# Attention and SwiGLU on one core: first head pair loaded as f32 over the hardware queues, three probability buffers, and a new order for the first sixth of the work list

## Chip, cores, metric

One core of a Trainium2 chip. The metric is the device time of one execution in microseconds. Profiles are one execution each, and their spans are about 2 us below the timed figures.

## The reference

Eight batches of causal attention (8 heads of 64, 576 tokens, 16 beacon keys that every token sees), whose output, heads side by side, goes through a SwiGLU block of width 1536.

```python
B, H, S, Nb, D = (8, 8, 576, 16, 64)
k_all = np.concatenate([beacon_k, k], axis=2)
v_all = np.concatenate([beacon_v, v], axis=2)
scores = scale * np.matmul(q, k_all.transpose(0, 1, 3, 2))      # causal mask on k, none on beacons
a = np.exp(scores - max); a /= a.sum(-1, keepdims=True) + 1e-09
x = np.matmul(a, v_all)                                          # -> (4608, 512)
g = x @ w_gate
out = (g * sigmoid(g) * (x @ w_val)) @ w_out
```

## The kernel before

All work is cut into pieces, and a string, the work list, gives their order of issue: `S` scores of half a head pair with their Exp, `P` probabilities times V for one head (PV), `K`/`Q` transposes of batch 0, `U` of batches 1 and 2, `X` transposes of the attention output, `g`/`G` quarters and whole units of the gate and value products, `F` one step of the output projection, `l` a load, `o` half of Wo, `c`/`d` a regrouping copy of a K or Q head pair of batch 0, `t` a DMA transpose, `w` four idle transposes. The same letter in the other case (`k`, `q`, `x`, `u`, `D`) is the same piece with its copy out on another engine; `g` and `G` alone differ in size. TensorE takes its part of the list strictly in order.

```python
pt = [static.tile([P, 2, P_W], BF16, name=f"p{i}") for i in range(2)]     # probabilities, by head pair m % 2
...
nc.vector.memset(pt[1][:, 0, 0:TOK], 0.0)
for h0, h1 in ((0, 2),):
    load_runs(nc.gpsimd, ks, k, 0, h0, h1)        # f32 in HBM -> bf16 in SBUF
    load_runs(nc.gpsimd, qs, q, 0, h0, h1)
nc.gpsimd.dma_start(beacons[:], beacon_k[0].rearrange("h j d -> j h d"))
make_identity(nc, ident)
...                                               # mask tile "below"
warm(13, TOK)                                     # 13 idle 128x512 matmuls
...
start = runs(2, 4) + runs(4, H) + v_loads(0, 0, H)   # then weights, batch 1
...
plan = [
    "llllllllllllllllllllllllllllllllllloo",
    "cdwwwwkQ",
    "ScDKSQ",
    "cDcDSKPSQP",
    "SKPXSQP",
    ...
```

From batch 2 on, the masks of the diagonal blocks are put on by GpSimd (`affine_select` on the probabilities after Exp), which also issues nearly all loads.

The softmax here doesn't subtract the row's maximum and nothing guards it: scores larger than these inputs give would overflow.

Of the kernel before, what the change touches and what calls it, by code (L numbers as in the profile page):

```python
# [10 lines left out]
BF16 = mybir.dt.bfloat16  # L11
FP32 = mybir.dt.float32

P = 128
S = 576
D = 64
NB = 16
NKT = 5
KPAD = NKT * P
TOK = 512  # L20
# [9 lines left out]
RP = S // ROWS  # L30

NHT = 2

PE_MASKS = (0, 1)

# [21 lines left out]
def kernel(  # L57
# [40 lines left out]

    QK = NKT * H * D
    QKP = ROWS * H * D  # L100
    qs = static.tile([P, QKP], BF16, name="qs")
    ks = static.tile([P, QKP], BF16, name="ks")
    beacons = static.tile([NB, H, D], BF16, name="beacons")
    qb = [static.tile([P, n], BF16, name=f"qb{i}") for i, n in ((0, QKP), (1, QK))]
    kb = [static.tile([P, n], BF16, name=f"kb{i}") for i, n in ((0, QKP), (1, QK))]
    vb = [static.tile([P, NKT, H, 68], BF16, name=f"vb{i}") for i in range(2)]
    qT = [static.tile([P, NPAIR, KPAD], BF16, name=f"qT{i}") for i in range(2)]
    kT = [static.tile([P, NPAIR, KPAD], BF16, name=f"kT{i}") for i in range(2)]
    pt = [static.tile([P, 2, P_W], BF16, name=f"p{i}") for i in range(2)]
    wg = static.tile([P, KD, DFF], BF16, name="wg")  # L110
    wv = static.tile([P, KD, DFF], BF16, name="wv")
    wo = static.tile([P, NF, DM], BF16, name="wo")
# [3 lines left out]
    def tiles(t):  # L116
        return t[:, 0:QK].rearrange("p (c h d) -> p c h d", c=NKT, d=D)

    def load_runs(eng, t, src, b, h0, h1):
        eng.dma_start(  # L120
            t[0:RP, ROWS * D * h0 : ROWS * D * h1].rearrange("p (h e) -> p h e", e=ROWS * D),
            src[b, h0:h1].rearrange("h (p i) d -> p h (i d)", i=ROWS),
        )

    loaded = {}
# [56 lines left out]
    def copy(eng, o, i):  # L182
        if eng is nc.scalar:
            nc.scalar.activation(o, i, ACT.Copy)
        else:
            nc.vector.tensor_copy(o, i)  # L186

    def transpose_pair(dst, src, n, m, pool, tag, eng):
        t_ps = pool.tile([P, KPAD], BF16, name="t_ps", tag=tag)
# [53 lines left out]
    def scores(b, m, units):  # L243

        on_pe = b in PE_MASKS
        tiles = {u: big.tile([P, 2, 512], FP32, name="s_ps", tag="big") for u in units}
        for u in units:
            for t, col, q0, n in UNITS[u][2]:
                for hh in range(2):
                    r = slice(64 * hh, 64 * hh + 64)  # L250
                    nc.tensor.matmul(  # L251
                        tiles[u][:, hh, col : col + n],
                        lhsT=kT[b % 2][r, m, P * t : P * t + P],
                        rhs=qT[b % 2][r, m, q0 : q0 + n],

                        start=not on_pe or col == 0,
                        stop=not on_pe,
                    )
        if on_pe:
            for u in units:  # L260
                for hh in range(2):
                    for col, n, d in UNITS[u][3]:
                        nc.tensor.matmul(  # L263
                            tiles[u][:, hh, col : col + n],
                            lhsT=below[:],
                            rhs=ident[:, d : d + n],
                            start=False,
                            stop=(col, n, d) == UNITS[u][3][-1],
                        )
        for u in units:  # L270
            c0, w, _, diagonals = UNITS[u]
            p = pt[m % 2]
            nc.scalar.activation(p[:, :, c0 : c0 + w], tiles[u][:, :, 0:w], ACT.Exp, scale=0.125)  # L273
            for col, n, d in [] if on_pe else diagonals:
                ap = p[:, :, c0 + col : c0 + col + n]
                nc.gpsimd.affine_select(  # L276
                    out=ap,
                    in_=ap,
                    compare_op=ALU.is_ge,
                    fill=0.0,  # L280
                    base=d,
                    pattern=[[0, 2], [1, n]],
                    channel_multiplier=-1,
                )
# [3 lines left out]
    def pv(b, m, hh, pool=att, tag="att"):  # L288
# [4 lines left out]
        for c, (q0, _) in enumerate(QBLOCKS):  # L293
            for t in range(c + 1):
                col = p_col(t, q0)
                nc.tensor.matmul(  # L296
                    o_ps[:, c, 0 : D + 1],
                    lhsT=pt[m % 2][:, hh, col : col + P],
                    rhs=vb[b % 2][:, t, h, 0 : D + 1],
                    start=(t == 0),  # L300
                    stop=(t == c),
                )
# [118 lines left out]


    nc.vector.memset(pt[1][:, 0, 0:TOK], 0.0)
    for h0, h1 in ((0, 2),):
        load_runs(nc.gpsimd, ks, k, 0, h0, h1)
        load_runs(nc.gpsimd, qs, q, 0, h0, h1)
    nc.gpsimd.dma_start(beacons[:], beacon_k[0].rearrange("h j d -> j h d"))
    make_identity(nc, ident)

    nc.gpsimd.memset(below[:], 0.0)  # L430
    nc.gpsimd.affine_select(
# [13 lines left out]
                idle[:, 0:cols], lhsT=pt[1][:, 0, 0:P], rhs=pt[1][:, 0, 0:cols], start=True, stop=True  # L445
            )

    warm(13, TOK)
    for i in range(2):
        nc.vector.memset(vb[i][:, :, :, D : D + 1], 1.0)  # L450
        nc.vector.memset(vb[i][64:P, 4, :, 0:D], 0.0)
        nc.vector.memset(kT[i][:, :, NB + S : KPAD], 0.0)
        nc.vector.memset(pt[i][:, :, 1664:P_W], 0.0)
    def kq_loads(b):

        k, q = k_loads(b, 0, H), q_loads(b, 0, H)
# [5 lines left out]



    done = dict.fromkeys("SPKQUXgGFcdltwo", 0)
    first = [(0, 0, 1), (0, 1, 2), (1, 0, 1), (1, 1, 2), (0, 2, 3), (1, 2, 3), (0, 3, 4), (1, 3, 4)]
    parts = [(j, *part) for j in range(2) for part in first]
    units = [(j, f) for j in range(NCH) for f in range(2 if j < 2 else 0, NF)]
# [11 lines left out]
    def kq_then(b):  # L480
        return [(load, b, False) for load in kq_loads(b)]

    def runs(h0, h1):
        return [lambda t=t, src=src: load_runs(nc.gpsimd, t, src, 0, h0, h1) for t, src in ((ks, k), (qs, q))]

    start = runs(2, 4) + runs(4, H) + v_loads(0, 0, H)
    for i in range(4):
        start += w_loads(i)
    start += k_loads(1, 0, H) + q_loads(1, 0, H) + v_loads(1, 0, H)
# [10 lines left out]
        return outp, "outp"  # L500

    def piece(kind):
        n = done[{"k": "K", "q": "Q", "u": "U", "x": "X", "D": "d"}.get(kind, kind)]
        eng = nc.scalar if kind in "kqx" else nc.vector
        if kind == "S":
            b, m = n // 8, n % 8 // 2
            assert done["P"] >= 2 * (n // 2) - 2
            if b == 0:
                assert min(done["K"], done["Q"]) > m
            else:  # L510
# [1 line left out]
            scores(b, m, ("AB", "DC" if b == 0 else "CD")[n % 2])  # L512
        elif kind == "P":
            b, m = n // 8, n % 8 // 2
            assert done["S"] >= 2 * (n // 2 + 1) and loaded[b, "v"] == 6
            pv(b, m, n % 2, *small())
            if b >= NPEX and n % 8 == 7:
                x_transpose(b)
# [3 lines left out]
                assert loaded[key] == (2 if key[1:] == (True, 0) else 1)  # L522
            transpose_both(bt, n % 4, (nc.scalar if kind == "u" else nc.vector, nc.vector))
        elif kind in "KkQq":
            assert done["c" if kind in "Kk" else "d"] > n
            turn = transpose_k if kind in "Kk" else transpose_q
            turn(n, *small(), eng)
        elif kind in "Xx":
# [18 lines left out]
        elif kind == "o":  # L547
            load_wo(n)
        elif kind == "w":
            spare.extend(range(4))  # L550
        elif kind == "c":
            assert done["l"] >= (0, 2, 4, 4)[n]
            regroup(kb[0], ks, n, nc.vector)
        elif kind in "dD":
            assert done["l"] >= (0, 2, 4, 4)[n]
            regroup(qb[0], qs, n, nc.scalar if kind == "d" else nc.vector)
        elif kind == "l":
            load, b, values = loads[n]
            assert free(b, values)
            load()  # L560
        elif kind == "t":
            assert done["S"] >= 8 * (n // 10 + NPE - 1)
            turns[n]()
        done[{"k": "K", "q": "Q", "u": "U", "x": "X", "D": "d"}.get(kind, kind)] += 1

    one_bank = [(outp, "outp")]
    two_banks = [(outp, "outp"), (att, "att")]
    plan = [
        "llllllllllllllllllllllllllllllllllloo",
        "cdwwwwkQ",  # L570
        "ScDKSQ",
        "cDcDSKPSQP",
        "SKPXSQP",
        "SPXSP",
        "gPgPgxXgg",
        "gggGGGGGUlGGGGUGllllll",
        "llF",
        "FFSFFS",
        "USPlFFlSPUFX",
        "lUSPFSPUFXlllFF",  # L580
        "SlPllllllFlSPUUtXFF",
        "lllllS",
        "tPggSPFFggXlgltgtPttlgtFlgGFt",
        "lltllGFSlFltFFFSllPlGlFG",
        "llSPFFGFllSPFlF",
        "GSFFFPGStFFPFGGtF",
        "PStFPFSGFFPFSlFFFFFFtStt",
        "lFllllFFltltP",
        "StFtSPGlPGFGG",
        "FPSFFlFlFFSFGlFFllPFGlFFS",  # L590
        "FPFFlFFSllFPFGGGlltlFtFtFt",
        "PSFlFFFtSFFFlFFlPGGlGFFFlFF",
        "tFPStFFlttFSFlPFFGlGGFFFlFlF",
        "SFPSFFlFtFFGPFGGFFFFFF",
        "lSllPFFFtSlllPFFGFGGFFFFFFttt",
        "ltFlSlPFFtFSllPFFGFGGFFFFFtttt",
        "llSPFFFSllPFFFGGGFFFFFF",
        "SllPFFFSPFFFGGGFFFFFF",
        "SPFFFSPFFFGGGFFFFFFttttt",
        "SPFFFSPFFFGGGFFFFFFttttt",  # L600
        "SllPFFFSllPFFFGGGFFFFFF",
        "SllPFFFSPFFFGGGFFFFFF",
        "SPFFFSPFFFGGGFFFFFF",
        "PFSFFFSPFFGFFGGFFFF",
        "SPFFFFSPFFGGFFFFF",
        "SPFFFFSPFGFFGGFFFFFF",
        "GFFPGFFFFGGPFFF",
        "GGFFFFFFFFFGFFFFFFFF",
        "FFFFFFFFFFFFFFF",
        "GFFFFFGFFFFGFGFFFFGFFFFFGFFFFFFFGFFFFGFFGFFGGFFF",  # L610
        "GFFFGFFGGFFGFFFFFFFFFFFFFGFFGFFFGFFFFFFFGFFGFFGFFFFFFGFFGFFF",
        "FFFFFFFFFFFFFFFFFFFFFFFFFFFFFFFFFFFFFFFFFFFFFFFFF",
    ]
    for kind in "".join(plan).replace(" ", ""):
        piece(kind)
    del done["w"]
    assert done == dict(S=8 * B, P=8 * B, K=4, Q=4, U=4 * (NPE - 1), X=4 * NPEX, g=16, G=len(units), F=4 * NF * NCH, c=4, d=4, o=2, l=len(loads), t=len(turns)), done


# [28 lines left out]
```

## Time and profile before

| | before |
|---|---|
| time, median (range) | 389.08 us (389.08 to 389.61, 3 runs) |
| span of the profiled run | 387.0 us |
| TensorE busy | 370.9 us (96%) |
| start of first useful transpose, first Exp | 7.67, 10.03 us |
| last PV of batch 0 ends | 31.4 us |
| first scores of batch 2 | 72.9 us |
| from there to the end | 314.1 us |

Times within a span are us from its first instruction. The lines behind these figures are in the prediction. The moment "first scores of batch 2" matters because the two work lists are the same from just before it.

### The profile page before, as it was taken

The numbers are of one execution on the slowest core, as the hardware profiler recorded it, in microseconds if no ns is written. First come the engines' busy times: TensorE is split into PE (matmuls) and PEld (weight loads), VectorE is DVE, ScalarE is ACT, GpSimd is POOL, SyncE is SP. The second block draws the span as 40 slices with busy tenths as digits, with TensorE's granted clock in tenths as the row PEclk, the third lists the DMA queues.
The fourth block names the chain that finished last, engine by engine and source line by source line (L and its number), as shares of the span: only waits on it lengthen the run. The fifth ranks groups of instructions, "written<-read, shape, count | busy, mean of one in ns | idle before, by whom it ended". The sixth has DMA issues, their size and how long they took to land.

```text
span 387.0 us, 7394 instructions
## 1 busy us (share of the span) xinstructions
PE 370.9 (96%) x2885; PEld 185.7 (48%) x2933; DVE 231.1 (60%) x430; ACT 169.2 (44%) x242; POOL 156.2 (40%) x270
## 2 busy tenths in 40 slices
PE   7799999999989999999999999999999999999996
PEld 3564446644445454454444444444444444444443
DVE  3456866575654666656666666665666636675652
ACT  2563346655565555555454455555552112222210
POOL 8847949589229676537633114311110000000000
PEclk9679999999999999999999999999999999999999
DMA  7999999999549999999995158722000311000013
GB/s 91 173 203 165 150 168 147 177 135 135 72 69 123 157 105 150 197 77 68 180 173 75 41 112 138 73 41 76 29 27 29 61 73 37 27 29 27 29 56 109
DMA packets 158660, 38.73 MB, mean 100 GB/s; under 512 B 146592, under 2 KB 154144, under 8 KB 158624
## 3 DMA queue, kind: packets, MB, share of 16 engines
q0 software_dynamic: 112864, 19.15, 67.6%
q1 hardware_dynamic: 45616, 19.03, 24.6%
q8 instruction: 23, 0.38, 0.4%
q14 instruction: 13, 0.11, 0.1%
q10 hardware_dynamic: 144, 0.07, 0.1%
HBM read 38.27 MB, written 9.44 MB: 123 GB/s over the span
## 4 chain that ended last, share of the span: by engine, by line
PE 90%; POOL 2%; ACT 2%; issue 2%; DMA 2%; DVE 2%; POOLq 0%; ACTq 0%
PE gv_ps L341 48%; PE o_ps L380 23%; PE pv_ps L296 8%; PE s_ps L251 7%; ACT p L273 2%; DMA vb<-in_v_dram 2%; PE t_ps L225 1%; PE s_ps L263 1%; POOL vb L130 1%; PE o_ps L400 1%; PE xt_ps L315 1%; POOL ks L120 1%; POOL qs L120 0%; DVE o_sb L389 0%; PE t_ps L200 0%
## 5 line engine op out<-in xcount | busy, mean ns | idle before, releaser
L354 ACT ACTIVATE th<-gv_ps 128x512 f32<-128x512 f32 x108 | 64.4, 597 | 160.1 <-PE gv_ps L341 158.5
L356 DVE SCALAR_TENSOR_TENSOR u<-th,gv_ps 128x512 f32<-128x512 f32 x108 | 74.2, 687 | 88.5 <-ACT th L354 88.0
L273 ACT ACTIVATE p<-s_ps 128x992 bf16<-128x992 f32 (+2 forms) x128 | 101.4, 864 | 35.9 <-PE s_ps L251 22.0
L341 PE MATMUL gv_ps<-xT,wg 128*128 128x512 bf16 x426 | 112.0, 379 | 0.5
L341 PE MATMUL gv_ps<-xT,wv 128*128 128x512 bf16 x419 | 110.8, 379 | 0.7
L380 PE MATMUL o_ps<-wo,hT 128*128 128x512 bf16 x391 | 103.9, 379 | 2.9 <-DVE o_sb L389 1.2
L276 POOL TENSOR_SCALAR_AFFINE_SELECT p<-p 128x256 bf16<-128x256 bf16 (+2 forms) x120 | 43.9, 391 | 111.3 <-ACT p L273 110.4
L359 DVE SCALAR_TENSOR_TENSOR hT<-gv_ps,u 128x512 bf16<-128x512 f32 x108 | 74.7, 691 | 3.7
L341 PEld LDWEIGHTS <-wv 128*128 128x128 bf16 x432 | 42.2, 98 | 50.2 <-issue 0.2
L341 PEld LDWEIGHTS <-wg 128*128 128x128 bf16 x432 | 41.6, 98 | 48.4 <-issue 1.3
L380 PEld LDWEIGHTS <-hT 128*128 128x128 bf16 x420 | 38.1, 98 | 43.5 <-issue 5.6
L296 PE MATMUL pv_ps<-vb,p 128*128 128x65 bf16 x960 | 41.8, 196 | 3.1 <-DVE x L305 1.3
L296 PEld LDWEIGHTS <-p 128*128 128x128 bf16 x960 | 36.1, 99 | 15.0 <-issue 6.5
L251 PE MATMUL s_ps<-qT,kT 64*128 64x80 bf16 (+4 forms) x384 | 36.6, 288 | 3.9 <-DVE qT L186 2.1
L130 POOL DMA_DIRECT2D kb<-in_k_dram x35 | 30.5, 871 | 8.4 <-DMA wv<-in_moe_w_val_dram 3.6
L130 POOL DMA_DIRECT2D vb<-in_v_dram x40 | 33.8, 859 | 0.0
L130 POOL DMA_DIRECT2D qb<-in_q_dram x35 | 30.5, 872 | 5.9 <-DMA wo<-in_moe_w_out_dram 3.0
L305 DVE TENSOR_TENSOR x<-pv_ps,rec 128x320 bf16<-128x320 f32 x64 | 31.5, 492 | 2.3
L304 DVE RECIPROCAL rec<-pv_ps 128x5 f32<-128x5 f32 x64 | 12.3, 192 | 33.9 <-PE pv_ps L296 33.6
L389 DVE COPY o_sb<-o_ps 128x512 f32<-128x512 f32 x35 | 24.0, 685 | 7.4 <-PE o_ps L380 7.4
L251 PEld LDWEIGHTS <-kT 64*128 64x128 bf16 x384 | 13.2, 95 | 27.4 <-issue 22.0
L186 DVE COPY qT<-t_ps 128x576 bf16<-128x576 bf16 x12 | 6.6, 551 | 5.6 <-PE t_ps L200 5.6
(51 smaller groups left out, 93.6 us busy)
## 6 DMA issues: line engine op xcount, KB each, us to landing
out_dram<-o_sb SPq DMA_DIRECT2D x35, 256.0 KB, 2.4
qb<-in_q_dram POOLq DMA_DIRECT2D x28, 128.0 KB, 6.0
vb<-in_v_dram POOLq DMA_DIRECT2D x24, 128.0 KB, 4.7
kb<-in_k_dram POOLq DMA_DIRECT2D x21, 128.0 KB, 6.5
wg<-in_moe_w_gate_dram POOLq DMA_DIRECT2D x4, 384.0 KB, 9.9
wv<-in_moe_w_val_dram POOLq DMA_DIRECT2D x4, 384.0 KB, 11.1
wo<-in_moe_w_out_dram POOLq DMA_DIRECT2D x2, 768.0 KB, 10.4
vb<-in_v_dram POOLq DMA_DIRECT2D x8, 112.0 KB, 4.7
```

The lines of the kernel that those rows point to most:

```text
L130: return eng.dma_start(dst[p0 : p0 + n, c, h0:h1, 0:D], src[b, h0:h1, r : r + n, :].rearrange("h j d -> j h d"))
L251: nc.tensor.matmul(tiles[u][:, hh, col : col + n], lhsT=kT[b % 2][r, m, P * t : P * t + P], rhs=qT[b % 2][r, m, q0 : q0 + n],  start=not o ...
L273: nc.scalar.activation(p[:, :, c0 : c0 + w], tiles[u][:, :, 0:w], ACT.Exp, scale=0.125)
L276: nc.gpsimd.affine_select(out=ap, in_=ap, compare_op=ALU.is_ge, fill=0.0, base=d, pattern=[[0, 2], [1, n]], channel_multiplier=-1,)
L296: nc.tensor.matmul(o_ps[:, c, 0 : D + 1], lhsT=pt[m % 2][:, hh, col : col + P], rhs=vb[b % 2][:, t, h, 0 : D + 1], start=(t == 0), stop=(t ...
L305: nc.vector.tensor_tensor(out=xs[b][:, :, D * h : D * h + D], in0=o_ps[:, :, 0:D], in1=rec[:].to_broadcast([P, NKT, D]), op=ALU.mult,)
L341: nc.tensor.matmul(gvs[f][:, TOK * half : TOK * half + TOK], lhsT=w[:, kk, P * f : P * f + P], rhs=xT[:, kk, r : r + TOK], start=(kk == 0) ...
L354: nc.scalar.activation(th[:], ps[:, 0:TOK], ACT.Tanh, scale=0.5)
L356: nc.vector.scalar_tensor_tensor(out=u[:], in0=th[:], scalar=1.0, in1=ps[:, 0:TOK], op0=ALU.add, op1=ALU.mult)
L359: nc.vector.scalar_tensor_tensor(out=hTs[j][:, f, :], in0=ps[:, TOK:1024], scalar=0.5, in1=u[:], op0=ALU.mult, op1=ALU.mult)
L380: nc.tensor.matmul(st["o"][:], lhsT=hTs[j][:, f, P * i : P * i + P], rhs=wo[:, f, :], start=(f == 0), stop=(f == NF - 1),)
L389: nc.vector.tensor_copy(o_sb[:], st["o"][:])
```

## The change

The intent: start attention sooner (the first K and Q need no issue on GpSimd; of two idle phases on TensorE one is shortened and one dropped), run scores and Exp ahead of PV (third buffer), and refit everything up to batch 2 around that.

```diff
+NPT = 3
-    pt = [static.tile([P, 2, P_W], BF16, name=f"p{i}") for i in range(2)]
+    pt = [static.tile([P, 2, P_W], BF16, name=f"p{i}") for i in range(NPT)]
+    beacons_in = static.tile([NB, H, D], FP32, name="beacons_in")
+    first_k = static.tile([RP, 2 * ROWS * D], FP32, name="first_k")
+    first_q = static.tile([RP, 2 * ROWS * D], FP32, name="first_q")
-    for h0, h1 in ((0, 2),):
-        load_runs(nc.gpsimd, ks, k, 0, h0, h1)
-        load_runs(nc.gpsimd, qs, q, 0, h0, h1)
-    nc.gpsimd.dma_start(beacons[:], beacon_k[0].rearrange("h j d -> j h d"))
+    for eng, t, src in ((nc.sync, first_k, k), (nc.scalar, first_q, q)):
+        eng.dma_start(t[:].rearrange("p (h e) -> p h e", h=2), src[0, 0:2].rearrange("h (p i) d -> p h (i d)", i=ROWS))
+    nc.sync.dma_start(beacons_in[:], beacon_k[0].rearrange("h j d -> j h d"))
+    load_runs(ks, k, 2, 4)
+    load_runs(qs, q, 2, 4)
     make_identity(nc, ident)
+    load_runs(ks, k, 4, H)
+    load_runs(qs, q, 4, H)
-    warm(13, TOK)
+    warm(9, TOK)
+    regroup(kb[0], first_k, 0, nc.vector)
+    nc.vector.tensor_copy(beacons[:], beacons_in[:])
+    regroup(qb[0], first_q, 0, nc.scalar)
     # "C": a Q regroup on GpSimd; "w" is gone
-        "llllllllllllllllllllllllllllllllllloo", "cdwwwwkQ", "ScDKSQ", "cDcDSKPSQP", "SKPXSQP", "SPXSP", ...
+        "llllllccclClqkcClllllkSQlllSKSlQKlSQSlllPPlSPlPl",
+        "SlXlPPllSoXglXgPPglloglgXgggGGlGlGGGlGGGuGlSlFlF", ...      # from "StPggSPFFgg" on as before
```

More of the change, by code (lines that the diff above doesn't have):

```diff
@@ L100 @@
     QKP = ROWS * H * D
+    beacons = static.tile([NB, H, D], BF16, name="beacons")
+    beacons_in = static.tile([NB, H, D], FP32, name="beacons_in")
     qs = static.tile([P, QKP], BF16, name="qs")
     ks = static.tile([P, QKP], BF16, name="ks")
-    beacons = static.tile([NB, H, D], BF16, name="beacons")
+    first_k = static.tile([RP, 2 * ROWS * D], FP32, name="first_k")
+    first_q = static.tile([RP, 2 * ROWS * D], FP32, name="first_q")
     qb = [static.tile([P, n], BF16, name=f"qb{i}") for i, n in ((0, QKP), (1, QK))]
@@ L117, in tiles, with load_runs @@
         return t[:, 0:QK].rearrange("p (c h d) -> p c h d", c=NKT, d=D)
-    def load_runs(eng, t, src, b, h0, h1):
-        eng.dma_start(
+    def load_runs(t, src, h0, h1):
+        nc.gpsimd.dma_start(
             t[0:RP, ROWS * D * h0 : ROWS * D * h1].rearrange("p (h e) -> p h e", e=ROWS * D),
-            src[b, h0:h1].rearrange("h (p i) d -> p h (i d)", i=ROWS),
+            src[0, h0:h1].rearrange("h (p i) d -> p h (i d)", i=ROWS),
         )
@@ L185, in copy @@
         else:
-            nc.vector.tensor_copy(o, i)
+            eng.tensor_copy(o, i)
     def transpose_pair(dst, src, n, m, pool, tag, eng):
@@ L271, in scores @@
             c0, w, _, diagonals = UNITS[u]
-            p = pt[m % 2]
+            p = pt[(NPAIR * b + m) % NPT]
             nc.scalar.activation(p[:, :, c0 : c0 + w], tiles[u][:, :, 0:w], ACT.Exp, scale=0.125)
@@ L297, in pv @@
                     o_ps[:, c, 0 : D + 1],
-                    lhsT=pt[m % 2][:, hh, col : col + P],
+                    lhsT=pt[(NPAIR * b + m) % NPT][:, hh, col : col + P],
                     rhs=vb[b % 2][:, t, h, 0 : D + 1],
@@ L446, in warm @@
             )
-    warm(13, TOK)
+    warm(9, TOK)
+    for i in range(NPT):
+        nc.vector.memset(pt[i][:, :, 1664:P_W], 0.0)
     for i in range(2):
@@ L452 @@
         nc.vector.memset(kT[i][:, :, NB + S : KPAD], 0.0)
-        nc.vector.memset(pt[i][:, :, 1664:P_W], 0.0)
+    regroup(kb[0], first_k, 0, nc.vector)
+    nc.vector.tensor_copy(beacons[:], beacons_in[:])
+    regroup(qb[0], first_q, 0, nc.scalar)
     def kq_loads(b):
@@ L457, in kq_loads @@
         return k[0:2] + q[0:1] + [load for c in range(1, NKT) for load in (k[c + 1], q[c])]
-    done = dict.fromkeys("SPKQUXgGFcdltwo", 0)
+    done = dict.fromkeys("SPKQUXgGFltwoc", 0)
     first = [(0, 0, 1), (0, 1, 2), (1, 0, 1), (1, 1, 2), (0, 2, 3), (1, 2, 3), (0, 3, 4), (1, 3, 4)]
@@ L481, in kq_then @@
         return [(load, b, False) for load in kq_loads(b)]
-    def runs(h0, h1):
-        return [lambda t=t, src=src: load_runs(nc.gpsimd, t, src, 0, h0, h1) for t, src in ((ks, k), (qs, q))]
-    start = runs(2, 4) + runs(4, H) + v_loads(0, 0, H)
+    start = v_loads(0, 0, H)
     for i in range(4):
@@ L502, in piece @@
     def piece(kind):
-        n = done[{"k": "K", "q": "Q", "u": "U", "x": "X", "D": "d"}.get(kind, kind)]
-        eng = nc.scalar if kind in "kqx" else nc.vector
+        n = done[{"C": "c", "k": "K", "q": "Q", "u": "U", "x": "X"}.get(kind, kind)]
+        eng = nc.scalar if kind in "kqx" else nc.gpsimd if kind == "C" else nc.vector
         if kind == "S":
             b, m = n // 8, n % 8 // 2
-            assert done["P"] >= 2 * (n // 2) - 2
+            assert done["P"] >= 2 * (n // 2) - 2 * (NPT - 1)
             if b == 0:
@@ L514, in piece @@
             b, m = n // 8, n % 8 // 2
-            assert done["S"] >= 2 * (n // 2 + 1) and loaded[b, "v"] == 6
+            assert done["S"] >= 2 * (n // 2 + 1) and loaded[b, "v"] == 6, (n, done, loaded)
             pv(b, m, n % 2, *small())
@@ L524, in piece @@
         elif kind in "KkQq":
-            assert done["c" if kind in "Kk" else "d"] > n
+            assert done["c"] >= 2 * n - (kind in "Kk")
             turn = transpose_k if kind in "Kk" else transpose_q
@@ L550, in piece @@
             spare.extend(range(4))
-        elif kind == "c":
-            assert done["l"] >= (0, 2, 4, 4)[n]
-            regroup(kb[0], ks, n, nc.vector)
-        elif kind in "dD":
-            assert done["l"] >= (0, 2, 4, 4)[n]
-            regroup(qb[0], qs, n, nc.scalar if kind == "d" else nc.vector)
+        elif kind in "cC":
+            m, i = n // 2 + 1, n % 2
+            regroup((kb, qb)[i][0], (ks, qs)[i], m, eng)
         elif kind == "l":
@@ L563, in piece @@
             turns[n]()
-        done[{"k": "K", "q": "Q", "u": "U", "x": "X", "D": "d"}.get(kind, kind)] += 1
+        done[{"C": "c", "k": "K", "q": "Q", "u": "U", "x": "X"}.get(kind, kind)] += 1
     one_bank = [(outp, "outp")]
@@ L568 @@
     plan = [
-        "llllllllllllllllllllllllllllllllllloo",
-        "cdwwwwkQ",
-        "ScDKSQ",
-        "cDcDSKPSQP",
-        "SKPXSQP",
-        "SPXSP",
-        "gPgPgxXgg",
-        "gggGGGGGUlGGGGUGllllll",
-        "llF",
-        "FFSFFS",
-        "USPlFFlSPUFX",
-        "lUSPFSPUFXlllFF",
-        "SlPllllllFlSPUUtXFF",
-        "lllllS",
-        "tPggSPFFggXlgltgtPttlgtFlgGFt",
-        "lltllGFSlFltFFFSllPlGlFG",
-        "llSPFFGFllSPFlF",
-        "GSFFFPGStFFPFGGtF",
-        "PStFPFSGFFPFSlFFFFFFtStt",
@@ L588 @@
-        "lFllllFFltltP",
-        "StFtSPGlPGFGG",
-        "FPSFFlFlFFSFGlFFllPFGlFFS",
-        "FPFFlFFSllFPFGGGlltlFtFtFt",
-        "PSFlFFFtSFFFlFFlPGGlGFFFlFF",
-        "tFPStFFlttFSFlPFFGlGGFFFlFlF",
-        "SFPSFFlFtFFGPFGGFFFFFF",
-        "lSllPFFFtSlllPFFGFGGFFFFFFttt",
-        "ltFlSlPFFtFSllPFFGFGGFFFFFtttt",
-        "llSPFFFSllPFFFGGGFFFFFF",
-        "SllPFFFSPFFFGGGFFFFFF",
-        "SPFFFSPFFFGGGFFFFFFttttt",
-        "SPFFFSPFFFGGGFFFFFFttttt",
-        "SllPFFFSllPFFFGGGFFFFFF",
@@ L602 @@
-        "SllPFFFSPFFFGGGFFFFFF",
-        "SPFFFSPFFFGGGFFFFFF",
-        "PFSFFFSPFFGFFGGFFFF",
-        "SPFFFFSPFFGGFFFFF",
-        "SPFFFFSPFGFFGGFFFFFF",
-        "GFFPGFFFFGGPFFF",
-        "GGFFFFFFFFFGFFFFFFFF",
-        "FFFFFFFFFFFFFFF",
-        "GFFFFFGFFFFGFGFFFFGFFFFFGFFFFFFFGFFFFGFFGFFGGFFF",
-        "GFFFGFFGGFFGFFFFFFFFFFFFFGFFGFFFGFFFFFFFGFFGFFGFFFFFFGFFGFFF",
-        "FFFFFFFFFFFFFFFFFFFFFFFFFFFFFFFFFFFFFFFFFFFFFFFFF",
+        "llllllccclClqkcClllllkSQlllSKSlQKlSQSlllPPlSPlPl",
@@ new lines @@
+        "SlXlPPllSoXglXgPPglloglgXgggGGlGlGGGlGGGuGlSlFlF",
+        "lFFlSUFuSPFSlPFlFuSPFFFFxSPlFSlllXFFlllllPUlSPUU",
+        "XlUtllllllStPggSPFFggXlgltgtPttlgtFlgGFtlltllGFS",
+        "lFltFFFSllPlGlFGllSPFFGFllSPFlFGSFFFPGStFFPFGGtF",
+        "PStFPFSGFFPFSlFFFFFFtSttlFllllFFltltPStFtSPGlPGF",
+        "GGFPSFFlFlFFSFGlFFllPFGlFFSFPFFlFFSllFPFGGGlltlF",
+        "tFtFtPSFlFFFtSFFFlFFlPGGlGFFFlFFtFPStFFlttFSFlPF",
+        "FGlGGFFFlFlFSFPSFFlFtFFGPFGGFFFFFFlSllPFFFtSlllP",
+        "FFGFGGFFFFFFtttltFlSlPFFtFSllPFFGFGGFFFFFttttllS",
@@ new lines @@
+        "PFFFSllPFFFGGGFFFFFFSllPFFFSPFFFGGGFFFFFFSPFFFSP",
+        "FFFGGGFFFFFFtttttSPFFFSPFFFGGGFFFFFFtttttSllPFFF",
+        "SllPFFFGGGFFFFFFSllPFFFSPFFFGGGFFFFFFSPFFFSPFFFG",
+        "GGFFFFFFPFSFFFSPFFGFFGGFFFFSPFFFFSPFFGGFFFFFSPFF",
+        "FFSPFGFFGGFFFFFFGFFPGFFFFGGPFFFGGFFFFFFFFFGFFFFF",
+        "FFFFFFFFFFFFFFFFFFGFFFFFGFFFFGFGFFFFGFFFFFGFFFFF",
+        "FFGFFFFGFFGFFGGFFFGFFFGFFGGFFGFFFFFFFFFFFFFGFFGF",
+        "FFGFFFFFFFGFFGFFGFFFFFFGFFGFFFFFFFFFFFFFFFFFFFFF",
+        "FFFFFFFFFFFFFFFFFFFFFFFFFFFFFFF",
@@ L616 @@
     del done["w"]
-    assert done == dict(S=8 * B, P=8 * B, K=4, Q=4, U=4 * (NPE - 1), X=4 * NPEX, g=16, G=len(units), F=4 * NF * NCH, c=4, d=4, o=2, l=len(loads), t=len(turns)), done
+    assert done == dict(S=8 * B, P=8 * B, K=4, Q=4, U=4 * (NPE - 1), X=4 * NPEX, g=16, G=len(units), F=4 * NF * NCH, o=2, c=6, l=len(loads), t=len(turns)), done
 _INS = ['q', 'k', 'v', 'beacon_k', 'beacon_v', 'moe_w_gate', 'moe_w_val', 'moe_w_out']
```

## The prediction

> **What bounds the kernel now.** I read the page first, then the windows of 2 us over the head, then the chain that ended last, the timeline of the head, and the timelines of each engine to 75 us. The page:
>
> ```profile
> PE 370.9 (96%) x2885; PEld 185.7 (48%) x2933; DVE 231.1 (60%) x430; ACT 169.2 (44%) x242; POOL 156.2 (40%) x270
> ...
> PE   7799999999989999999999999999999999999996
> ...
> PEclk9679999999999999999999999999999999999999
> DMA  7999999999549999999995158722000311000013
> ```
>
> TensorE is the bound: 9 in nearly every slice, 16 us idle in all (387.0 - 370.9). Two things stand out at the left edge. The granted clock is 6 in the second slice, so its "busy" is partly slow work. And the DMA engines are full from about 5 to 97 us. The windows show the first point more closely (columns: width, busy us of each engine, then clock, DMA share, GB/s):
>
> ```profile
> 10.00:12.00 2.00, 1.69 (x29) 1.29 (x27) 0.83 (x2) 1.97 (x3) 1.76 (x3) 1.00 1.37 151
> 12.00:14.00 2.00, 1.15 (x10) 0.38 (x8) 1.47 (x4) 1.16 (x2) 0.88 (x2) 0.79 2.33 158
> 14.00:16.00 2.00, 1.47 (x16) 1.03 (x14) 1.61 (x4) 1.83 (x2) 2.00 (x3) 0.50 2.15 167
> 16.00:18.00 2.00, 1.27 (x14) 0.87 (x15) 0.20 (x1) 0.00 (x0) 2.00 (x4) 0.50 1.39 200
> ```
>
> From about 13.5 to 22.7 us the clock is at one half, and at 16 to 18 us ScalarE does nothing at all. The chain that ended last says why (start, us, what):
>
> ```profile
> 8.31 2.71 POOL vb L130 x3
> 11.02 6.48 DMA vb<-in_v_dram
> 17.54 0.22 PE pv_ps L296
> 17.76 0.70 PE s_ps L251 x7
> ```
>
> The probabilities-times-V product of head pair 0 stands in TensorE's in-order queue ahead of the next scores, and V lands only at 17.5 us, issued last behind six other loads on GpSimd. The start of the timeline:
>
> ```profile
> 4.75 0.39 DVE L186 COPY kb<-ks 96x768 bf16<-96x768 bf16 x1 [1.89 <-DMA ks<-in_k_dram]
> 5.44 0.84 ACT L184 ACTIVATE qb<-qs 96x768 bf16<-96x768 bf16 x1 [3.35 <-DMA qs<-in_q_dram]
> 6.58 1.06 PE L194 MATMUL t_ps<-ident,below 128*128 128x128 bf16 x16
> 7.67 0.43 PE L200 MATMUL t_ps<-ident,kb 96*128 96x96 bf16 x6
> 9.21 0.58 PE L251 MATMUL s_ps<-qT,kT 64*128 64x496 bf16 x4 [0.85 <-DVE qT L186]
> 10.03 3.13 ACT L273 ACTIVATE p<-s_ps 128x992 bf16<-128x992 f32 x4 [1.17 <-PE s_ps L263]
> 18.82 1.41 ACT L273 ACTIVATE p<-s_ps 128x416 bf16<-128x416 f32 x2 [2.85 <-PE s_ps L263]
> ```
>
> K arrives at 4.75 and Q at 5.4, but TensorE runs 13 idle matmuls to 6.7 and 16 idle transposes to 7.64; useful work starts at 7.67, the first Exp at 10.0. The last line merges two Exps, the first waiting 2.85 us for scores held behind V.
>
> **What the Trainium skill says.** "TensorE: Matmul & The Clock Gate", Part 1 (The HAM clock gate): the array runs at half rate until a free-running window of about 3.4 us has been busy, and falls back after an idle one. The trace agrees in kind: the idle matmuls start 427 ns apart (5.47 us for 13) and the idle transposes take 66 ns each, so full speed came near 6.6 us; and with TensorE only about 60% busy in 12 to 14 us it fell to half. "DMA: Bandwidth & Descriptors", section "SWDGE vs HWDGE vs iDMA": a cast needs the GpSimd queue, a plain copy can use the SyncE or ScalarE queue with quicker setup; hence f32 tiles and a cast in the regroup copy. Before, the GpSimd loads of one head pair took 3.1 to 3.3 us from issue to landing; SyncE stores of 256 KB took 2.4. "GPSIMD Engine Reference", section 4.1, puts one-input copies there near line rate; no GpSimd copy is in this trace. "VectorE: DVE Perf Modes", Mode 2x_1P, wants 16-bit data, so the f32 regroup loses the packed rate: 0.39 us now, I estimate 0.9 (the f32 eviction of 512 elements took 0.685, so 768 take about 1.0 from PSUM, a little less from SBUF).
>
> **The change part by part.** Comparing the two work lists, the last 746 pieces are the same; only what comes before the first scores of batch 2 is reordered, with the same pieces. Those scores start at 72.9 us. So the question is how far that moment moves.
>
> Floor of the stretch at full clock, start-to-start from the timeline: 16 score pieces of 0.72 (11.5), 14 PV of 0.45 (6.3), 4 K of 0.35 and 4 Q of 0.27 (2.5), 8 double transposes of 0.65 (5.2), 6 x transposes of 0.28 (1.7), 12 FFN units of 1.73, two of them in quarters (20.8), 15 projection steps of 0.216 (3.2): 51.2 us. Before it took 72.9 - 7.67 = 65.2. So 14 us are lost: about 3.6 to the half clock (half of some 7.3 busy us in 13.5 to 22.7), the rest to waits, nearly all in batch 0 (its last PV ends at 31.4) and some 3 at 54 to 65, where TensorE waits for Exp.
>
> - Early start. The f32 loads go out near 0.8 us from SyncE and ScalarE; with 2.4 us for 256 KB and two transfers side by side I take 3.0: landed at 3.8. Regroup to 4.8, beacon copy to 5.3, ScalarE's Q to 4.7. Nine idle matmuls end at 1.26 + 9 x 0.427 = 5.1. No idle transposes. Useful work from 5.2 instead of 7.67: **2.5 us**. The first three evictions (q, k, next k) all go on ScalarE, 0.65 to 0.75 each, so the first Exp comes at about 8.6, 1.4 us sooner.
> - Exp no longer held. Five score pieces now come before the first PV, which three probability buffers allow. A pair of score pieces costs ScalarE 3.24 us (1.83 for the first two Exps, 1.41 for the other two, by the merged rows of its timeline), so four pairs need 13.0: from 8.6 the batch's Exps end at 21.6 if nothing interrupts, against 30.0. I add 1 us for V (GpSimd issues it about 2 us earlier, landing near 15.5 to 16) and 1.9 for a clock that will still fall, since K, Q and two score pieces are only 2.06 us of TensorE in 3.24: Exps end at 24.5, last PV at about 25.4 instead of 31.4.
> - The rest of the stretch. Behind that lie some 2.6 (remaining quarters), 0.3, and 15.6 (nine units) to the first transposes of batch 1: 44. From there to the first scores of batch 2 the pieces add to 19.2; eight score pieces need 13 us of ScalarE there, so 2 us of waiting for Exp stay: **65.3**. Gain at that moment 72.9 - 65.3 = 7.6.
> - Moved: two Q regroups go to GpSimd (about 1 us each by estimate) while its queue is full anyway; 0.84 of the Q cast stays on ScalarE; memsets of a third buffer 0.1. Beside other work, cost nothing.
> - Later on the list is unchanged and TensorE-bound, so the shift carries; the third buffer gives nearly nothing (no wait for a probability buffer is among the large waits). I take 0.5 off for later places where loads or ScalarE are then less far ahead. Sum: 389.1 - 7.1 = **382.0 us**.
>
> **The rivals.** (1) *Loads become the bound.* The DMA engines are full to 97 us. Moved bytes (as written in bf16) before Wo's second half and V of batch 1 are there: 8.26 MB, which the GB/s row sums to at about 52 us; K and Q of batch 2 (9.44 MB) at about 60. The queue now runs perhaps 1.5 us earlier, so these are there at 50.5 and 58.5; by my walk projection needs the second half of Wo at 53 and the batch-2 transposes come at 60. It just fits, so no more than 1 to 1.5 us beyond my figure can be won, and if the start is not earlier some 2 us are lost: 384. (2) *The clock stays cold.* Nine warm-ups end before the speed-up seen near 6.6 us. If TensorE stays at half rate from 5 to about 22 us, batch 0's 12 us of work take 24 and end near 29: a gain of 3 to 4, 385.5. For it: about 60% occupancy was too little before. Against: slow work fills the window and brings the clock back, as it did at 22.7. (3) *All of it works*: clock held, V early, first batch-2 scores at 62.5: gain 10, 379. (4) *Handed back*: the fixed part was tuned to the old timing and swallows half: 385. Slower needs a new stall of over 15 us; nothing points there.
>
> **Range and chances.** Weights of about 0.45 for my walk (380.5 to 383), 0.25 for the full success (378 to 380.5) and 0.3 for rivals 1, 2, 4 (383.5 to 386) give 382.0 with 378.0 to 386.0. The 2% line is 381.3, just below my centre: faster 0.43, same 0.54, slower 0.03.
>
> **What would show it.** Right: the first K or Q transpose at about 5.2, first Exp near 8.6, no ScalarE wait of 2.85 us before V, batch 0's last PV near 25, first batch-2 scores near 65, and the distance from there to the end as before (314 us). Wrong: f32 landings after 4.5 us; clock at 0.5 until past 20 us; TensorE waiting for Wo, V or K loads between 44 and 65; or the distance to the end grown by over 2 us.

## The result

The changed kernel takes 382.58 us (median of 4 runs, 382.54 to 382.80) against 389.35 (389.08 to 389.70) beside it. The ratio is 0.9824, 95% interval 0.9804 to 0.9843. Page of the changed kernel, the same rows as the prediction quotes:

```profile
PE 366.1 (96%) x2865; PEld 183.2 (48%) x2913; DVE 228.9 (60%) x424; ACT 172.4 (45%) x248; POOL 156.5 (41%) x269
...
PE   6999999999899999999999999999999999999996
...
PEclk9799999999999999999999999999999999999999
DMA  9999999999279999939994359431000310000012
```

TensorE is still 9 nearly everywhere and still the bound; the low clock is still in the second slice, and the DMA engines are now full from the very start. Windows of 2 us (width, busy us by engine, then clock, DMA share, GB/s):

```profile
6.00:8.00 2.00, 1.17 (x17) 0.92 (x18) 1.01 (x3) 1.48 (x4) 2.00 (x4) 0.91 1.30 182
8.00:10.00 2.00, 2.00 (x18) 1.07 (x17) 0.99 (x2) 1.28 (x4) 2.00 (x3) 0.50 1.76 169
...
14.00:16.00 2.00, 2.00 (x35) 1.69 (x33) 1.31 (x3) 1.97 (x3) 2.00 (x4) 0.88 1.25 186
```

The half-clock stretch came earlier and was shorter: two windows of 3.41 us by the clock record, from 7.65 to 14.5 us, where before it had been three, 13.2 to 23.4 (the prediction read 13.5 to 22.7 off the windows). The start of the timeline:

```profile
5.42 0.56 DVE L191 CAST kb<-first_k 96x768 bf16<-96x768 f32 x1 [2.50 <-DMA first_k<-in_k_dram]
5.67 0.84 ACT L189 ACTIVATE qb<-first_q 96x768 bf16<-96x768 f32 x1 [3.11 <-DMA first_q<-in_q_dram]
6.57 0.43 PE L205 MATMUL t_ps<-ident,qb 96*128 96x96 bf16 x6 [1.74 <-ACT qb L189]
9.74 1.83 ACT L278 ACTIVATE p<-s_ps 128x992 bf16<-128x992 f32 x2 [0.49 <-PE s_ps L268]
14.03 6.18 ACT L278 ACTIVATE p<-s_ps 128x992 bf16<-128x992 f32 x8 [0.87 <-PE s_ps L268]
16.88 1.07 PE L301 MATMUL pv_ps<-vb,p 128*128 128x65 bf16 x30
```

K and Q land *later* than before (5.4 and 5.7 against 4.75 and 5.4), useful work starts 1.1 us earlier and the first Exp only 0.3 us. But then eight Exps run in one block from 14.0 to 20.2, and the first two PV pieces come at 16.9 with no wait at all, where before TensorE stood at V until 17.5 and ScalarE behind it.

The lead can be followed through the list, because the pieces are the same. Starts of the Exp of a few score pieces, in us, from the traces (piece 1 to 8 are batch 0, 9 to 16 batch 1, 17 to 24 batch 2; "+13" has 13 idle matmuls):

| kernel | 1st | 8th | 17th | 25th | span |
|---|---|---|---|---|---|
| before | 10.03 | 28.58 | 73.40 | 107.17 | 387.0 |
| changed | 9.74 | 22.80 | 65.83 | 100.72 | 380.8 |
| changed, second profile | 9.36 | 23.83 | 66.86 | 101.09 | 381.2 |
| before, f32 pair only | 8.98 | 26.71 | 71.22 | 104.98 | 385.1 |
| before, third buffer only | 8.94 | 28.25 | 73.41 | 107.12 | 387.2 |
| before, less idle work | 9.18 | 27.81 | 76.07 | 109.83 | 389.6 |
| changed, first pair on GpSimd | 9.75 | 24.16 | 67.19 | 101.62 | 381.4 |
| changed, two buffers | 10.08 | 25.12 | 68.22 | 102.50 | 382.6 |
| changed +13 | 9.08 | 20.88 | 64.79 | 100.25 | 380.4 |
| +13, two buffers | 8.95 | 22.10 | 65.19 | 100.54 | 380.6 |
| +13, first pair on GpSimd | 9.20 | 23.50 | 66.52 | 101.08 | 380.9 |
| +13, GpSimd loads later | 9.31 | 21.11 | 64.18 | 101.57 | 381.7 |
| +13, loads moved | 9.18 | 20.99 | 64.02 | 100.30 | 380.4 |
| +13, more loads moved | 9.49 | 21.29 | 65.26 | 99.69 | 380.8 |

Before against changed, the lead is 0.3 us at the first piece, 5.8 at the eighth, 7.6 at the seventeenth and 6.45 at the twenty-fifth; at the end 6.2 are left. How well such starts repeat can be read from the table too: the two profiles of the changed kernel differ by 1.03 us at the eighth and seventeenth piece, and the last two kernels, whose lists are the same up to there, by 1.24 at the seventeenth. So a difference of this size in one profile is put down to an edit only where the wait behind it is found in the trace.

### The profile page after: what moved, and what is told of

It is laid out like the page before. It is cut to its first block, busy times and chain, and to the rows that moved or that the text cites. A ratio compares the mean times of both kernels' runs of the same rounds, so it can differ in the third digit from the quotient of the medians.

```text
span 380.8 us, 7356 instructions
## 1 busy us (share of the span) xinstructions
PE 366.1 (96%) x2865; PEld 183.2 (48%) x2913; DVE 228.9 (60%) x424; ACT 172.4 (45%) x248; POOL 156.5 (41%) x269
## 4 chain that ended last, share of the span: by engine, by line
PE 91%; ACT 2%; DVE 2%; issue 1%; DMA 1%; POOL 1%; ACTq 0%; POOLq 0%
PE gv_ps L346 49%; PE o_ps L385 22%; PE pv_ps L301 8%; PE s_ps L256 7%; PE s_ps L268 1%; PE t_ps L230 1%; ACT p L278 1%; DMA first_q<-in_q_dram 1%; PE t_ps L205 1%; PE o_ps L405 1%; PE xt_ps L320 1%; POOL p L281 0%; DVE o_sb L394 0%; DVE u L361 0%; DVE hT L364 0%
## 5 line engine op out<-in xcount | busy, mean ns | idle before, releaser
L278 ACT ACTIVATE p<-s_ps 128x992 bf16<-128x992 f32 (+2 forms) x128 | 101.5, 864 | 27.1 <-PE s_ps L256 22.7
L281 POOL TENSOR_SCALAR_AFFINE_SELECT p<-p 128x256 bf16<-128x256 bf16 (+2 forms) x120 | 43.8, 395 | 102.8 <-ACT p L278 102.8
L301 PE MATMUL pv_ps<-vb,p 128*128 128x65 bf16 x960 | 39.6, 193 | 1.9 <-DVE x L310 1.3
L301 PEld LDWEIGHTS <-p 128*128 128x128 bf16 x960 | 34.5, 97 | 14.0 <-issue 5.3
L256 PE MATMUL s_ps<-qT,kT 64*128 64x80 bf16 (+4 forms) x384 | 36.3, 289 | 1.1 <-DVE hT L364 0.3
L256 PEld LDWEIGHTS <-kT 64*128 64x128 bf16 x384 | 13.2, 95 | 22.7 <-issue 19.6
## 6 DMA issues: line engine op xcount, KB each, us to landing
wv<-in_moe_w_val_dram POOLq DMA_DIRECT2D x4, 384.0 KB, 10.2
```

The source lines that it names most:

```text
L256: nc.tensor.matmul(tiles[u][:, hh, col : col + n], lhsT=kT[b % 2][r, m, P * t : P * t + P], rhs=qT[b % 2][r, m, q0 : q0 + n],  start=not o ...
L278: nc.scalar.activation(p[:, :, c0 : c0 + w], tiles[u][:, :, 0:w], ACT.Exp, scale=0.125)
L281: nc.gpsimd.affine_select(out=ap, in_=ap, compare_op=ALU.is_ge, fill=0.0, base=d, pattern=[[0, 2], [1, n]], channel_multiplier=-1,)
L301: nc.tensor.matmul(o_ps[:, c, 0 : D + 1], lhsT=pt[(NPAIR * b + m) % NPT][:, hh, col : col + P], rhs=vb[b % 2][:, t, h, 0 : D + 1], start=( ...
```

## The experiments

Theory A: the gain is the new order of batch 0, helped by loads that stand earlier in the GpSimd queue; an earlier landing of the first pair is no part of it. Main rival: the f32 load itself. Beside these stood the questions of the clock, and of where a lead is lost again.

**The f32 pair alone, in the old order.**

```diff
-        load_runs(nc.gpsimd, ks, k, 0, h0, h1)
-        load_runs(nc.gpsimd, qs, q, 0, h0, h1)
+    (the three f32 loads over SyncE and ScalarE; regroup from first_k, first_q, and a copy of the beacons)
```

> The kernel before with only the f32 load of the first head pair over the SyncE and ScalarE queues; order, buffers and idle work as before. Theory A: the first useful transpose stays at 7.67 us (idle work before it), V lands 1 to 2 us earlier than 17.5, so the wait for V shrinks and the total falls by 1 to 2 us, to about 387.5. Rival (the load is a main part of the gain): 385.5 or less.

Measured: 387.68 us, ratio 0.9959 (0.9931 to 0.9987). That is the 1 to 2 us expected (the first Exp came 1.05 us earlier all the same, for in this run the clock rose to full at 4.1 us, not 6.3, and the idle transposes were over sooner; the run with the third buffer alone shows the same). What shrank is the wait for V. PV of head pair 0 in the kernel before, then in this one:

```profile
16.36 0.38 PE L296 MATMUL pv_ps<-vb,p 128*128 128x65 bf16 x4 [0.62 <-DMA vb<-in_v_dram]
17.01 0.75 PE L296 MATMUL pv_ps<-vb,p 128*128 128x65 bf16 x6 [0.27 <-DMA vb<-in_v_dram]
```

```profile
14.50 0.38 PE L299 MATMUL pv_ps<-vb,p 128*128 128x65 bf16 x4 [0.77 <-DMA vb<-in_v_dram]
15.18 0.70 PE L299 MATMUL pv_ps<-vb,p 128*128 128x65 bf16 x6 [0.31 <-DMA vb<-in_v_dram]
```

The last part of V comes 1.8 us sooner, because two loads and the beacons no longer stand ahead of it on GpSimd, and the fourth score piece's Exp moves by 1.9 us (18.82 to 16.95).

**The third buffer alone, and less idle work alone.** The first edit takes `pt[(4 * b + m) % 3]` in the old order; the second drops `wwww` and four idle matmuls.

> The kernel before with three probability buffers and nothing else. Theory A (the third buffer is worth something only because the new order makes use of it): same time as before within 0.5 us. Rival (Exp had been waiting for a free buffer along the whole list): 1 us or more faster.

> The kernel before without the 16 idle transposes and with 9 idle matmuls in place of 13. Theory A (V is what ends the first stretch, so an earlier first transpose buys little): first useful transpose at 6.3 us instead of 7.67, but PV still waits for V to 17.5, total within 0.7 us of before, or slower if the clock comes down earlier. Rival (the idle work at the start costs its full 1.3 us): 387.7 or less.

Measured: 389.09 us, 0.9971 (0.9946 to 0.9996), and 389.19 us, 0.9974 (0.9945 to 1.0004), beside runs of the kernel before that spread from 388.8 to 391.7. At most 0.55% each. By medians both are 1.0 to 1.1 us faster, not within the 0.5 and 0.7 us that theory A gave, and the first interval just leaves out 1; so the times alone don't refute the rival of the third buffer. The table speaks against it: leads of 0.3 and 0.8 us at the eighth piece don't last. With the third buffer the 17th and 25th pieces stand where they stood, within 0.05 us; with less idle work the profiled run had even lost 2.7 us by piece 17 (2.29 of it in one wait for a K load of batch 2, of which I don't know why it came late). That profile doesn't price the idle work at full clock: its first useful transpose came at 5.88 us, but the clock record has it at half to 20.8 us and again from 65.2 to 68.6. Neither edit is where the 6.8 us come from.

**The new order with the first pair on GpSimd again.**

```diff
-    (the three f32 loads)
+    load_runs(ks, k, 0, 2)
+    load_runs(qs, q, 0, 2)
+    nc.gpsimd.dma_start(beacons[:], beacon_k[0].rearrange("h j d -> j h d"))
```

> The changed kernel, but the first head pair of K and Q and the beacons come as bf16 over the GpSimd queue again, ahead of the other loads, as in the kernel before. Theory A (the order of the work and the third buffer bring the gain; the f32 load itself brings no earlier landing, since K and Q landed at 5.4 and 5.7 us against 4.75 and 5.4 before, and is worth only the 2 us of GpSimd issue that it frees): first K and Q at 4.7 and 5.4 us, the first useful transpose at about 6.3, V about 1.5 us later, total 383 to 384.5. Rival (the f32 load is a main part of the gain): total 385 or more.

Measured: 383.56 us, 0.9854 (0.9821 to 0.9886). The first pair landed at 4.7 and 5.4 us, as with the old kernel, and the first Exp started at 9.75, the same as with f32. So about five sixths of the gain (1 - 0.9854 against 1 - 0.9824; by the intervals 1.1 to 1.8% against 1.6 to 2.0%) stay without the f32 load: the rival falls. In the profile the later loss, 1.4 us by the eighth piece, goes with a half clock that lasted to 18.0 instead of 14.5, so against this profile the load can't be priced. The second profile of the changed kernel is the better partner, since its clock record is the same (half from 7.80 to 18.04 us in both): there the kernel with the f32 load is ahead by 0.39 us at the first piece, 0.33 at the eighth and seventeenth, 0.53 at the twenty-fifth and 0.2 at the end.

**The new order with two buffers.** The only reordering this needs:

```diff
-NPT = 3                      +NPT = 2
-  ...KlSQSlllPPlSPlPl        +  ...KlSQPPSllllSPlPl
```

> The changed kernel with two probability buffers; the only reordering this forces is that the first two PV pieces come before the fifth score piece instead of after it. Theory A (scores must not stand behind the wait for V): V lands near 16 us, so the fifth score piece and its Exps wait until about 17 to 18 and total is 1 to 2.5 us above the changed kernel, about 384. Rival (V is early enough by now and the third buffer idle ballast): within 0.5 us of 382.6.

Measured: 383.73 us (382.12 to 384.31), 0.985 (0.982 to 0.988). This run taught me to distrust the clock row. Its column reads 1.00 throughout, yet the same four score matmuls took

```profile
13.04 0.98 PE L256 MATMUL s_ps<-qT,kT 64*128 64x496 bf16 x4
...
18.53 0.58 PE L256 MATMUL s_ps<-qT,kT 64*128 64x496 bf16 x4
```

0.98 us at 13 and 0.58 at 18.5. The record holds only changes; before the first one the row shows 1.00. Here the array ran at half speed from the start to the first recorded change, at 16.5 us, so the loss (2.3 us at the eighth piece) is in part the clock's. The question had to be asked again at full clock.

**Thirteen idle matmuls.**

```diff
-    warm(9, TOK)
+    warm(13, TOK)
```

> The changed kernel with 13 idle matmuls in place of 9. The page shows TensorE idle from 4.8 to 6.57 us and the clock at one half from about 7.6 to 14.5. Theory C (that idle stretch is what brings the clock down): 13 matmuls end near 6.7, the clock stays full at least until about 11, and the total falls by 0.5 to 2 us, to about 381. Rival (the thin work in 7 to 14 us brings it down in any case, and Exp is the limit there): clock down 3.4 us later or not at all changed, total within 0.4 us of 382.6.

Measured: 381.77 us (381.13 to 383.69), 0.9816 (0.9782 to 0.9850). In the profile no half-clock stretch is left in batch 0: four score matmuls take 0.58 from 8.3 us on, Exps run without a gap over 0.2 us from 9.08 to 18.3, and piece 8 comes 1.9 us sooner than in the changed kernel. Theory C holds for the clock: with this order all four profiles with nine idle matmuls have a half-clock stretch in batch 0, and of the five with thirteen and the f32 pair (four follow below) none has. Its forecast of the time is not shown: by medians the kernel is 0.8 us faster, but the ratios, 0.9816 and 0.9824, hardly differ. In the profile only 0.4 of the 1.9 us are left at the end. Where they went:

```profile
46.59 1.02 PE L385 MATMUL o_ps<-wo,hT 128*128 128x512 bf16 x3 [1.11 <-DMA wo<-in_moe_w_out_dram]
...
71.79 0.36 PE L301 MATMUL pv_ps<-vb,p 128*128 128x65 bf16 x6 [0.33 <-POOL p L281]
```

The first projection step waits for Wo, which was issued at 37.05 us, only 0.2 us sooner than in the changed kernel (37.22): TensorE is early, the loads are not. Near 70 us PV waits for masks on GpSimd, and between pieces 17 and 19 the rest of the lead is gone.

**At full clock: two buffers; first pair on GpSimd; GpSimd loads held back.** The last builds identity and mask ahead of the first GpSimd load, so that the f32 loads start alone.

> The changed kernel with 13 idle matmuls (which kept the clock full in its profile) and two probability buffers, the first two PV pieces moved ahead of the fifth score piece. Same question as the earlier two-buffer run, whose clock was low in the profiled run, so that the effect could not be told apart. Theory A (third buffer lets scores run ahead of the wait for V): at full clock V is there by about 15 us and the fifth piece could run at 14.2, so its Exps come 1 to 1.5 us later than the 15.13 of the 13-matmul kernel; at the end 0.3 to 1 us is left. Rival: fifth piece no later, total equal within 0.3 us.

> The changed kernel with 13 idle matmuls and the first head pair as bf16 over the GpSimd queue. Theory A: first K and Q as early as with f32 (within 0.4 us), first Exp within 0.4 us, but all later loads 1 to 2 us later, so the wait for Wo near 46 us grows from 1.1 to some 2.5 and the total is 1 to 2 us above the 13-matmul kernel. Rival (where the first pair comes from does not matter): within 0.4 us.

> The changed kernel with 13 idle matmuls, and GpSimd builds the identity and the mask before it issues its first load, so that the f32 loads have the DMA engines to themselves for about 1 us more. Theory D (the f32 loads took 4.6 to 4.8 us because the GpSimd loads share the engines): they land at least 0.6 us earlier, first Exp some 0.5 us earlier than 9.08, later loads about 1 us later. Rival (4.6 us is what such a load costs by itself, with its 192 rows of 1536 bytes): landing within 0.2 us of before.

Measured on one chip: 381.74 us, 0.9818 (0.9793 to 0.9842); 383.65 us, 0.9843 (0.9822 to 0.9864); 383.25 us, 0.9841 (0.9822 to 0.9860).

The third buffer: the fifth piece's Exp starts at 16.38 instead of 15.13, 1.25 us later, as forecast, but not for the reason forecast. PV started at 13.95 and found V there; its only wait was for another copy:

```profile
14.96 0.61 PE L301 MATMUL pv_ps<-vb,p 128*128 128x65 bf16 x15 [0.39 <-DVE qT L191]
```

So the buffer saves the time of two PV pieces ahead of the scores, not a wait for V. Of the 1.2 us at the eighth piece 0.3 are left at the 25th, and the times tie (0.9818 against 0.9816): that the third buffer gains anything at the end is not shown.

The first pair on GpSimd: the first Exp is 0.12 us later, but the later Q and K pairs land later, TensorE waits for their copies three times (0.34 to 0.50 us), and the third piece comes 0.9 us later; then the clock fell to half for 3.4 us. This looks like no chance: all five runs of this kernel have a mean clock of 0.985 to 0.994, those of the other kernels with thirteen 0.998 to 1.000 (though such a mean can hide a slow start, as above). By the ratios the total is about 1 us above the two-buffer kernel beside it, the low end of what theory A gave; the intervals overlap. The wait for Wo that was to grow disappeared, since TensorE no longer came early.

GpSimd loads held back: the f32 loads took from issue to landing, in the changed kernel and in this one,

```profile
first_q<-in_q_dram ACTq DMA_DIRECT2D x1, 288.0 KB, 4.8
first_k<-in_k_dram SPq DMA_DIRECT2D x1, 288.0 KB, 4.6
```

```profile
first_q<-in_q_dram ACTq DMA_DIRECT2D x1, 288.0 KB, 4.7
first_k<-in_k_dram SPq DMA_DIRECT2D x1, 288.0 KB, 4.5
```

They land no sooner, but this edit did not test theory D: it moved the first GpSimd issue from 1.38 to only 1.84 us, and the first GpSimd packet not at all (4.02, against 4.06 with thirteen matmuls alone). What speaks against the theory are the packets of the changed kernel: issue at 0.82, first packet at 1.86, last at 4.83, consumer at 5.4 us, while the GpSimd queue's first packet comes only at 3.93, when 341 of the 384 rows of the two loads had been started. So sharing with GpSimd can have slowed the last rows alone; how much the two loads slow each other was not tested. It is the GpSimd loads that come later beside the f32 loads: the first is issued at 1.38 us in both kernels, and its first packet comes at 3.93 here, at 2.83 in the kernel before. The kernel with loads held back then waits four times for masks, 0.33 to 0.68 us each, and ends slower; what brings these waits on is not shown.

**Moving loads so that the lead is kept.** On top of 13 idle matmuls: the first half of Wo ahead of V of batch 1, and five loads of batch 3 behind the first two score pieces of batch 2.

```diff
-  SlXlPPllSoXg...   UtllllllStPggSPFFgg
+  SloXlPPllSXg...   UtlStPggSPlllllFFgg
```

> The changed kernel with 13 idle matmuls, the first half of Wo loaded ahead of V of batch 1, and five loads of batch 3 moved behind the first two score pieces of batch 2, so that their masks on GpSimd do not stand behind DMA issues. Theory E (the 1.9 us that the 13 matmuls gain in batch 0 are lost again to a wait for Wo, 1.1 us at 46.6, and to masks waiting behind DMA issues near 70, about 1.2 us): both waits vanish and the total falls by about 1.5 us against the 13-matmul kernel, to 379 to 380.5. Rival (the loads as a whole are the bound there): the wait moves to V or to K and Q of batch 2 and the total stays within 0.5 us.

Measured: 382.15 us (381.44 to 383.17), 0.9820 (0.9798 to 0.9842): the total stays, as the rival said, but not for its reason. Both waits vanished, and at the 19th piece this kernel was 2.0 us ahead of the 13-matmul one (75.48 against 77.47). At the 24th it was level. TensorE's wait, and GpSimd at the same time:

```profile
91.31 0.29 PE L301 MATMUL pv_ps<-vb,p 128*128 128x65 bf16 x4 [1.21 <-POOL p L281]
```

```profile
89.30 0.73 POOL L135 DMA_DIRECT2D vb<-in_v_dram  x1
90.31 0.53 POOL L135 DMA_DIRECT2D kb<-in_beacon_k_dram  x1 [0.28 <-DMA kb<-in_k_dram]
90.84 1.04 POOL L281 TENSOR_SCALAR_AFFINE_SELECT p<-p 128x256 bf16<-128x256 bf16 x3
```

The mask of 90.84 belongs to an Exp that had ended at 86.75; it stood behind DMA issues of 0.5 to 0.9 us each in GpSimd's queue.

**Five more loads moved**, to behind the last score piece of batch 2.

> As the tuned run before it, and five more loads (K and Q of batch 4, V of batch 3) moved from between the score pieces of batch 2 to behind its last one, where GpSimd was idle from 96.6 to 101.4 us. Theory F (a lead on TensorE is eaten by masks that stand behind DMA issues on GpSimd: the lead of 1.8 us at the 19th score piece was gone at the 24th, after 1.5 us of PV waiting for masks): that wait vanishes, the lead stays, total about 1.5 us below the tuned run, 380 to 381. Rival (something else sets the pace there, V of batch 3 for one): a new wait near 102 to 105 us and the total within 0.5 us of the tuned run.

> The changed kernel unaltered, to have it on the same chip as the tuned version and with more runs: 382 to 384 us, depending on where the half-clock stretch falls; ratio to the kernel before 0.980 to 0.986.

Measured on one chip: 382.26 us (380.79 to 382.62), 0.9781 (0.9754 to 0.9808), and for the changed kernel unaltered 383.31 us (381.94 to 384.45), 0.9818 (0.9790 to 0.9846). In the profile the 1.2 us of masks are gone, and the 25th piece is the earliest of all kernels (99.69): from the 17th to the 25th it took 34.4 us, the tuned run 36.3. But I had moved V of batch 3 too far:

```profile
106.19 0.19 PE L301 MATMUL pv_ps<-vb,p 128*128 128x65 bf16 x1 [0.68 <-DMA vb<-in_v_dram]
```

and from the 25th piece to the end it took 281.1 us against 280.1. So theory F holds for the masks, and the rival's new wait came as well. On the total they stay undecided: by medians this kernel is level with the tuned one (382.26 and 382.15), by ratios 0.4% better, and the two were measured on different chips. This is the best ratio, some 0.4% below the changed kernel's on the same chip; the intervals overlap, so that it beats it is likely and not shown.

## Why the prediction was right

The time (382.0 predicted, 382.58 measured) and the central moment (first batch-2 scores 65.3 predicted, 65.32 measured) were right, partly by luck, because errors cancelled: of its own signs of being wrong one came true, f32 landings after 4.5 us. Step by step:

- *Early start, 2.5 us*: the mis-sized term. I put the f32 landing at 3.8 us, from a single SyncE store of 256 KB in 2.4 us; two loads at once took 4.6 to 4.8. Useful work came at 6.57 (5.2 predicted), the first Exp at 9.74 (8.6). The regroup was overestimated: 0.56 us for 768 elements in f32 (0.34 to 0.41 in bf16), not 0.9. "VectorE: DVE Perf Modes" has, besides the 16-bit mode that I cited, a two-port mode (Mode 2x_2P) for copies of one source within SBUF, which would fit; no run here tests it. What the load does bring is one step further on: the GpSimd queue issues K, Q and V of the rest sooner, worth 1.3 us by medians in the old order (before_f32). In the new one it is about 1 us by ratios, but 0.2 to 0.5 where two profiles have the same clock record; the rest goes with the clock.
- *Exp no longer held*: right in kind, and the new order is the bulk: without the f32 load it keeps about five sixths of the gain, with two buffers as much (0.985). But the order is one bundle (PV behind more scores, copies on other engines, loads spread out, less idle work), and no run takes it apart or takes load and buffer away together; that the place of PV is its main part is read from the traces, where ScalarE's wait of 2.85 us is gone. From the first Exp to the end of batch 0's last I had 15.9 us (8.6 to 24.5); it took 14.5 (9.74 to 24.2), so my allowances for V and clock, 2.9 us, were too large by 1.4, and this repaid the late start. The third buffer's part was forecast as room to run past the wait for V; at full clock V was already there and it was worth two PV pieces.
- *Clock*: "will still fall" was right: 6.8 us at half against 10.2. But I named the thin work in batch 0 as the reason; four more idle matmuls removed it in the profile, so in this kernel it is the idle stretch from 4.8 to 6.57 us that brings the clock down, a stretch that would not exist had the f32 pair landed when I said. Both reasons come down to how busy TensorE was in the 3.41 us before the fall: 1.50 us in the changed kernel (4.23 to 7.65), while with thirteen matmuls it was 2.46 and the clock stayed. Thin work can do it too: with the first pair on GpSimd as well, TensorE was busy 2.31 us from 11.20 to 14.61 and the clock fell. No threshold comes out of this: with thirteen matmuls the clock stayed full through 2.24 us of 3.41 at 45.4.
- *The rest of the stretch*: last PV of batch 0 at 25.2 (25.4), first batch-1 transposes at 43.8 (44), batch-2 scores at 65.3 (65.3).
- *Moved*: the two Q regroups on GpSimd took 0.84 us each (about 1 predicted).
- *What is handed back*: 0.5 predicted; from there to the end it took 315.5 us against 314.1, so 1.4, of which 1.1 lie between the 17th and the 25th piece. The largest waits there are 0.40 us for an Exp (66.87) and 0.33 for masks on GpSimd (92.36), a queue I had in view only as one with room to spare; the second profile has no such wait for masks and handed back 0.8. The rest is not explained. Rival 1 (loads) is not the bound of the changed kernel, but it is what the faster ones ran into: Wo at 46.6, K and Q of batch 2 at 60, V of batch 3 at 106.
- *Rival 2*: the clock's phase (where its steps of 3.41 us fall) differs from run to run: the changed kernel's second profile had 10.2 us at half, piece 8 came 1.0 us later, and 0.4 us was left of that at the end.

Open: how much of each run's spread is the clock's phase (only profiled runs show when it changes), whether the last variant's advantage is real, and which part of the new order gives how much.

## What to carry to other kernels

In a kernel bound by one in-order engine, look for the piece that stands in the queue in front of ready work: the new order, which moves it, was worth more here than taking the first pair off the GpSimd queue. A lead gained at the start is only kept if every queue behind it has room: check the loads, and the queue that both issues loads and does compute, before paying for more lead. Follow the same few pieces through both traces; the table of their starts showed where a lead was lost when the totals could not. Compare profiles with the same clock record, and look for the wait itself: the same kernel's starts moved by 1.0 us between two profiles.

## What the Trainium skill lacked or had wrong

- "DMA: Bandwidth & Descriptors", Specifications, gives the hardware path a first-byte latency of about 0.6 us; here the first packet came 1.04 us after the start of the issue instruction and 0.64 after its end. The page doesn't say from where it counts, so this shows a gap and no error. Its fit in "Anatomy of one DMA" is for the GpSimd path; taken over for these two loads of 295 KB together (my estimate from that fit: 2.0 + 590/436 = 3.4 us) it would fall short of the 4.6 to 4.8 us measured.
- "TensorE: Matmul & The Clock Gate", Part 1, agrees that the clock is half or full only, and in steps of 3.41 us (6.83 and 10.24 us at half in two profiles of the same kernel). Its table has the fall after an idle window; here it came after windows that were not idle, 44% busy in the changed kernel and 66% in the kernel before (9.76 to 13.18). It says the ramp is under 1% of a span and not to be fitted; that holds here too (0.4 us of 381 at the end), but effects of 1 us can't be read without it: one step more at half moved the eighth score piece by 1.0 us. No page I read says that the profile's clock row reads full before the first recorded change (score matmuls of 0.98 us at "1.00").
- "Trainium Kernel Development and Optimization", Key Constraints, says several issuing engines only save issue time. That time was the cost here: 0.5 to 0.9 us per GpSimd issue, with a mask 4.1 us behind the Exp that fed it (90.84 against 86.75 us).
